# Layer 1 of a two-layer attention and Fourier kernel: token blocks 2 and 3 arrive transposed from the host instead of being turned by TensorE

## The chip, the core and the metric

The kernel runs on one core of a Trainium2 chip. The metric is the device time of one execution in microseconds (us). TensorE is called PE here, as in the profile; its weight loads are PEld. VectorE is DVE, ScalarE is ACT, GpSimd is POOL, SyncE is SP.

## What is computed

The input is one sequence of S = 2048 tokens with D = 640 features, float32, and it goes through two equal layers. With 32 heads of 20 features, one layer is

```python
x = x + attention(layernorm(x)) @ wo     # q, k, v = layernorm(x) @ wqkv
x = x + fourier(layernorm(x))            # y = Real(DFT_seq(DFT_hidden(x)))
```

`layernorm` subtracts a token's mean and divides by its standard deviation; there is no learned scale.

## The kernel before, in words

A layer has a prologue (`Qkv.prologue`, L293), an attention sweep, an output projection and a Fourier stage. The change lies in the prologue of the first layer, which takes the first 86 us.

The prologue makes what attention needs to begin: for every token the first chunk of q and k (128 of 640 columns each) and the first half of v. A product contracts over the features, so both operands need the features on the partitions. The tokens come with tokens on the partitions and must be turned. They are handled in four blocks of 512, called tb = 0 to 3, each in five chunks of 128 features, dc = 0 to 4. Float32 is kept by splitting each operand into a high and a low part: `split` (L85) lets ACT copy the source to the rounded high part (L90), and DVE then subtracts that from the source to get the low part (L91). A product of one chunk is three passes: high by high, high by low, low by high (`passes`, L100).

How a block gets ready: `load` (L146) brings 256 tokens as one tile `xa`, two for a block. `stats` (L153) lets DVE take means and variances (L121 to L124) and POOL take the power and the product (L125, L126), so that the row scale and the row bias stand in `ars`, one number per token, tokens on partitions. `norm` (L156) lets ACT normalize in place, once per 128 tokens (L130). `turn` (L164) lets PE transpose 128x128 pieces into PSUM (L167), four for a chunk, 20 for a block, and splits each chunk into `xt`.

Each engine works strictly through its own queue in the order in which the code issues to it (the schedule is manual), and waits where an operand isn't ready. The loop at L346 sets that order. For block tb it issues: the k and q products of the block (`pqk`, L103, 15 passes each; `keep` evicts them by ACT at L218 and DVE at L220 and L221 and stores them by a POOL DMA at L222); `stats` for a block further on; `turn(tb + 1)`; loads and `norm` for block tb + 2; the norms (`pn`, L230 and L231); and last, from tb = 1 on, the 60 passes of v (`pv`, L103), evicted by ACT at L263. In block 0 the v passes come ahead of `turn(1)`. So for blocks 2 and 3 the operands `xt` are made while PE works on the v passes of the block before, and PE reads them in the order dc = 0, 1, 2, 3, 4 as soon as those end. PSUM has eight banks, handed out in rotation by `bank` (L160).

SP issues the loads in the same order; after the loads of block 3 it issues the reads of q and k for the first attention step (L519, L520, L505, L506). `ones(t)` (L325) writes ones into the v tiles by POOL; the v tiles 12 to 15 are last to be used.

Of the kernel before, what the change touches and what calls it, by code (L numbers as in the profile page):

```python
# [5 lines left out]
F32 = mybir.dt.float32  # L6
F32R = mybir.dt.float32r
# [3 lines left out]
OP = mybir.AluOpType  # L11
# [25 lines left out]


@with_exitstack
def mha_fnet_kernel(ctx, tc, x_in, wqk, wv, wo, seq, hid, nat_seq, nat_hid, out):  # L40
    nc = tc.nc
    V, A, G, PE = nc.vector, nc.scalar, nc.gpsimd, nc.tensor

# [92 lines left out]
    class Qkv:  # L136
# [27 lines left out]
        def turn(s, tb, wait=False):  # L164
# [9 lines left out]
            for dc in range(ND):  # L174
# [95 lines left out]
        def begin(s, first, kq, vals, room, given):  # L270


            s.first, s.room, s.given, s.w = first, room, given, {}
# [19 lines left out]
        def prologue(s, vals, xt, fill, att):  # L293
# [31 lines left out]
            def ones(t):  # L325
                s.v[t] = vals(f"v{t}", [H * VW + 12], F32, "v")
                G.memset(s.v[t][:, :H * VW].rearrange("p (a c) -> p a c", c=VW)[:, :, DH:], 1.0)
                G.memset(s.v[t][:, H * VW:], 1.0)

            for t in range(NT - ND):  # L330
                ones(t)
            def later(tb, k, f):
                if tb + 2 < NB:
                    f(2 * tb + 4 + k)
# [11 lines left out]
            for tb in range(NB):  # L346

                sq, late, last = {}, tb == 0, tb == NB - 1
                if late:
                    for k in range(2):  # L350
                        later(tb, k, s.load)
                for k in (1, 0) if last else (0, 1):
                    p = s.bank([128, 512], "pqk")
                    for dc in range(ND):
                        for f in s.product(p, s.w[k], tb, dc):
                            f()
                    sq[k] = s.keep(p, k * ND, tb, False, (room, fill)[k])
                    if late:
                        s.stats(2 + k)
                        continue  # L360
                    later(tb, k, s.stats)
                if late:
                    for n in range(4):
                        own(tb, n)
                        if n < 2:
                            s.norm(2 + n)
                            later(tb, n, s.stats)
                if tb == 0:
                    att.setup()
# [1203 lines left out]
        banks(None)  # L1573


_INS = ["x", "wqk", "wv", "wo", "seq", "hid", "nat_seq", "nat_hid"]
_OUTS = [((S, D), "float32")]


# [16 lines left out]
def _laid_out(A_x, A_wqkv, A_wo, B_dft_seq_re, B_dft_seq_im, B_dft_hid_re, B_dft_hid_im):  # L1596
    import numpy as np

    so, do = _orders()
    w = np.asarray(A_wqkv)[do]  # L1600
    nat_seq = np.stack([np.asarray(B_dft_seq_re), np.asarray(B_dft_seq_im)])[:, so][:, :, so]
    nat_hid = np.stack([np.asarray(B_dft_hid_re), np.asarray(B_dft_hid_im)])[:, do][:, :, do]
    seq = nat_seq.reshape(2, NB, 512, NT // 2, 2, 128).transpose(1, 0, 3, 5, 4, 2)
    return {
        "x": np.asarray(A_x).reshape(S, D)[so][:, do],
        "wqk": w[:, :2 * D].reshape(ND, 128, 2 * ND, 128).transpose(2, 1, 0, 3),
        "wv": w[:, 2 * D:].reshape(ND, 128, D),
        "wo": np.asarray(A_wo)[:, do].reshape(ND, 128, D),
# [1 line left out]
        "hid": nat_hid.transpose(0, 2, 1),  # L1610
        "nat_seq": nat_seq,
        "nat_hid": nat_hid,
    }


# [23 lines left out]
```

## Time and profile before

| what | value |
|---|---|
| device time, median of 3 runs | 2447.79 us (2447.61 to 2448.09) |
| device time of the profiled execution | 2448.03 us |
| its span in the trace | 2446.2 us |
| PE busy from 8 to 86 us | 77.3 of 78 us |
| DVE busy from 8 to 86 us | 41.7 of 78 us |
| ACT busy from 8 to 86 us | 41.1 of 78 us |
| POOL busy from 8 to 86 us | 14.8 of 78 us |
| PE busy over the whole span | 99% |
| ACT busy over the whole span | 86% |

A row of the timeline reads: start in us, length in us, engine, source line, operation, output and inputs by the program's names, how many instructions are merged into the row, and in brackets how long the engine was idle before it and what ended the wait. The length of a merged row runs from the first start to the last end. A row of the groups reads: busy us in all, mean ns of one, idle time before. "SPq" is SP's queue: the length there is the time to issue, not to transfer.

### The profile page before, as it was taken

How to read it: one execution, taken by the hardware profiler on the slowest of the kernel's cores; microseconds unless marked ns; L12 is line 12 of the kernel's file. 1: busy time of each engine (PE TensorE's matmuls, PEld its weight loads, DVE VectorE, ACT ScalarE, POOL GpSimd, SP SyncE). 2: the span in 40 equal slices, each digit the busy share in tenths (PEclk: the TensorE clock that was granted, in tenths of full speed). 3: DMA queues.
4: the chain of work that ended last, by engine and by line, in shares of the span. 5: the costliest groups of instructions: out<-in, count | busy, mean ns of one | idle time of the engine just before them, and what ended most of it. 6: DMA issues, size and time to landing. Idle time of an engine off the chain costs nothing. (4 is left out here: it accounts for less than half of the span.)

```text
span 2446.2 us, 43822 instructions
## 1 busy us (share of the span) xinstructions
PE 2423.5 (99%) x16320; PEld 1168.3 (48%) x16320; DVE 995.9 (41%) x2246; ACT 2115.4 (86%) x2428; POOL 528.8 (22%) x1032
## 2 busy tenths in 40 slices
PE   8999999999999999999999999999999999999998
PEld 7644444443333332339895444454433333333496
DVE  6244442234333433427753444323433332333275
ACT  6699998899999999995457999988999999999862
POOL 2012211112212122115321212211111211222143
PEclk9999999999999999999999999999999999999999
DMA  5324231223222225318552332312221322252265
GB/s 185 101 89 127 81 113 51 77 71 108 73 93 89 89 91 162 102 39 294 188 189 96 111 103 85 118 54 70 77 83 57 92 63 70 57 153 76 77 242 198
DMA packets 128226, 262.63 MB, mean 107 GB/s; under 512 B 29936, under 2 KB 54288, under 8 KB 128004
## 3 DMA queue, kind: packets, MB, share of 16 engines
q1 hardware_dynamic: 89412, 159.89, 20.1%
q0 software_dynamic: 38592, 99.85, 12.8%
q8 instruction: 131, 2.15, 0.4%
q14 instruction: 91, 0.75, 0.1%
HBM read 175.29 MB, written 84.31 MB: 106 GB/s over the span
## 5 line engine op out<-in xcount | busy, mean ns | idle before, releaser
L544 ACT ACTIVATE e<-psc 128x1024 f32<-128x1024 f32 x2048 | 1918.0, 1060 | 108.6 <-PE psc L541 98.2
L552 PE MATMUL acc<-e,v 128*32 128x512 f32 x8192 | 1030.0, 600 | 0.4 <-DVE of L559 0.4
L541 PE MATMUL psc<-stq,stk 62*128 62x512 f32 x4096 | 746.9, 445 | 1.9 <-ACT e L544 0.5
L541 PEld LDWEIGHTS psc<-stq,stk 62*128 62x128 f32 x4096 | 334.1, 184 | 705.0 <-ACT e L544 567.5
L552 PEld LDWEIGHTS acc<-e,v 128*32 128x32 f32 x8192 | 211.1, 108 | 407.3 <-issue 369.4
L103 PE MATMUL pqk<-xt,wqk 128*128 128x512 f32 x1200 | 319.6, 407 | 0.0
L573 POOL DMA_DIRECT2D o<-oh x256 | 131.5, 522 | 825.7 <-DVE oh L568 814.0
L88 DVE CAST hl<-pqk 128x512 fp32r<-128x512 f32 x64 | 44.3, 692 | 603.4 <-PE pqk L103 603.4
L103 PEld LDWEIGHTS pqk<-xt,wqk 128*128 128x128 f32 x1200 | 213.5, 188 | 83.2 <-issue 39.6
L103 PE MATMUL pv<-wv,xt 128*128 128x320 f32 x960 | 151.7, 313 | 0.0
L103 PEld LDWEIGHTS pv<-wv,xt 128*128 128x128 f32 x960 | 141.0, 188 | 13.5 <-issue 9.7
L559 DVE STREAM_TRANSPOSE of<-acc 128x512 f32<-128x512 f32 x64 | 45.8, 715 | 226.3 <-PE acc L552 226.3
L573 POOL DMA_DIRECT2D o<-ot x256 | 128.6, 509 | 1.8 <-issue 0.9
L222 POOL DMA_DIRECT2D scrk<-hl x40 | 27.8, 694 | 412.5 <-DVE hl L91 251.9
L222 POOL DMA_DIRECT2D scrq<-hl x40 | 28.3, 708 | 404.9 <-DVE hl L91 239.8
L96 PE MATMUL py<-wo,o 128*128 128x320 f32 x320 | 101.0, 315 | 0.0
L822 DVE TENSOR_REDUCE far<-cq 128x1 f32<-128x512 f32 (+5 forms) x169 | 98.5, 584 | 5.7
L98 PE MATMUL py<-wo,o 128*128 128x320 f32 x320 | 98.7, 308 | 0.0
L97 PE MATMUL py<-wo,o 128*128 128x320 f32 x320 | 98.7, 308 | 0.0
L826 DVE TENSOR_TENSOR cq<-cq 128x512 f32<-128x512 f32 (+4 forms) x166 | 96.4, 581 | 3.7 <-DMA cq<-in_nat_seq_dram 3.3
L261 DVE COPY v<-pv 128x320 f32<-128x320 f32 x32 | 15.7, 489 | 161.2 <-PE pv L103 161.2
L231 DVE TENSOR_REDUCE top<-pn 32x1 f32<-32x512 f32 x50 | 33.7, 676 | 76.7 <-PE pn L230 76.5
(204 smaller groups left out, 1758.5 us busy)
## 6 DMA issues: line engine op xcount, KB each, us to landing
cq<-in_nat_seq_dram POOLq DMA_DIRECT2D x64, 512.0 KB, 5.3
scrq<-hl POOLq DMA_DIRECT2D x40, 512.0 KB, 3.2
scrk<-hl POOLq DMA_DIRECT2D x40, 512.0 KB, 3.1
stq<-scrq SPq DMA_DIRECT2D x256, 80.0 KB
stk<-scrk SPq DMA_DIRECT2D x128, 160.0 KB
o<-o SPq DMA_DIRECT2D x32, 384.0 KB
stq<-scrq SPq DMA_DIRECT2D x256, 40.0 KB
stk<-scrk SPq DMA_DIRECT2D x128, 80.0 KB
```

Source lines behind the costliest of these rows:

```text
L96: PE.matmul(out_ap, ah, bh, start=start, stop=False)
L97: PE.matmul(out_ap, ah, bl, start=False, stop=False)
L98: PE.matmul(out_ap, al, bh, start=False, stop=stop)
L103: yield lambda i=i, j=j, k=k: PE.matmul(out_ap, a[i], b[j], start=dc == 0 and k == 0, stop=dc == ND - 1 and k == 2)
L222: G.dma_start(s.scr["qk"[k]][c * 128:(c + 1) * 128, :, tb * 512:(tb + 1) * 512], hl.bitcast(F32))
L541: PE.matmul(p[:, i], s.k[g, kc // 8, j][r, kc % 8 * 128:(kc % 8 + 1) * 128], s.q[g, qb, j][r], start=True, stop=True)
L544: A.activation(e, p, AF.Exp, scale=SCALE)
L552: PE.matmul(s.acc[32 * j:32 * j + 32], s.a.v[kc][:, v0:v0 + 32], s.e[n, j // 2][:, j % 2], start=kc == 0, stop=kc == NT - 1, skip_group_ch ...
L559: V.transpose(t0.rearrange("p b c -> p (b c)"), s.acc)
L573: G.dma_start(s.o[k, h * DH:(h + 1) * DH, qb * 512:(qb + 1) * 512], hl[k][32 * j:32 * j + DH])
L822: V.tensor_reduce(to, x, op=OP.max, axis=AX.X, apply_absolute_value=True)
L826: V.tensor_tensor(y, x, y, op=op)
```

## The change

The host adds an input `x_turned`, the tokens of the second half of the sequence (blocks 2 and 3), with features on the first axis. In the first layer only (`host`, which is true where the source is the input `x_in`), blocks 2 and 3 are no longer normalized by ACT and turned by PE.

- `row` (new, in the place of `norm` for blocks 2 and 3): SP writes the row scales and biases of the block to DRAM, four DMAs of 256 single numbers, then reads them back spread over all 128 partitions as two tiles `row` of 512 numbers each, then loads the block's part of `x_turned` by four DMAs into the two tiles that had held the block's tokens (1.3 MB for a block; the tokens themselves are still loaded for the statistics).
- `spread` (new, in the place of `turn(2)` and `turn(3)`): for each chunk POOL multiplies by the scale row, DVE adds the bias row, ACT copies the high part, DVE subtracts for the low part. The fifth chunk lies in two halves of 256 tokens, so a block has six steps.
- The `row` tiles live where v tiles 12 to 15 will be, so the ones for these four are written after block 3 is spread.

```diff
+        def row(s, k):
+            tb, j = divmod(k, 2)
+            if j == 0:
+                s.stat = dr.tile([2, 512], F32, name=f"stat{tb}_{s.L}")
+            for i in range(2):
+                nc.sync.dma_start(s.stat[i, j * 256:(j + 1) * 256].rearrange("(n p) -> p n", p=128), s.rs[k][:, i],
+                                  single_packet=False)
+            if j == 0:
+                return
+            s.rows = [s.vals(f"v{NT - 1 - 2 * (tb - 2) - i}", [512], F32, "row") for i in range(2)]
+            for i in range(2):
+                nc.sync.dma_start(s.rows[i], s.stat[i:i + 1].to_broadcast([128, 512]))
+            s.turned = [(s.first if n % 4 < 2 else s.room)(f"x{n % 4}", [2 * D], F32, "xturned") for n in (k - 1, k)]
+            src = x_turned.rearrange("c p t -> p c t")[:, :, (tb - 2) * 512:(tb - 1) * 512]
+            for i, t in enumerate(s.turned):
+                nc.sync.dma_start(t[:, :1024].rearrange("p (c t) -> p c t", c=2), src[:, 2 * i:2 * i + 2])
+                nc.sync.dma_start(t[:, 1024:], src[:, ND - 1, i * 256:(i + 1) * 256])
+
+        def spread(s, tb):
+            for dc in range(ND):
+                x = s.xtp(f"xt{tb}_{dc}", [2, 512], F32R, "xt")
+                s.xt[tb, dc] = [x[:, 0], x[:, 1]]
+                whole = [(s.turned[dc // 2][:, dc % 2 * 512:(dc % 2 + 1) * 512], slice(0, 512))] if dc < ND - 1 else \
+                    [(t[:, 1024:], slice(256 * i, 256 * i + 256)) for i, t in enumerate(s.turned)]
+                for y, cols in whole:
+                    G.tensor_tensor(y, y, s.rows[0][:, cols], op=OP.mult)
+                    V.tensor_tensor(y, y, s.rows[1][:, cols], op=OP.add)
+                    split(x[:, 0, cols], x[:, 1, cols], y)
...
                 elif tb == 1:
-                    for t in range(NT - ND, NT):
+                    for t in range(NT - ND, NT - 4 if host else NT):
                         ones(t)
                 if tb + 1 < NB:
-                    s.turn(tb + 1)
+                    (s.spread if host and tb else s.turn)(tb + 1)
                     for k in range(2):
                         later(tb + 1, k, s.load)
+                if tb == 2 and host:
+                    for t in range(NT - 4, NT):
+                        ones(t)
                 for k in range(1 if last else 0, 2):
-                    later(tb, k, s.norm)
+                    later(tb, k, s.row if host else s.norm)
                     s.norms(s.bank, k * ND, tb, sq[k])
```

In the changed kernel the lines behind the new functions are 31 to 36 higher (L222 is L253, L263 is L294). Three places show how the queues change.

DVE, where block 2 is made ready (behind the statistics of block 3, ahead of the evictions of block 2), before:

```order
L123 TENSOR_SCALAR ars<-amv 128x2
L124 TENSOR_SCALAR ars<-amv 128x2
L91 TENSOR_TENSOR xt<-ptr,xt 128x512 x5
L231 TENSOR_REDUCE top<-pn 32x1
L221 TENSOR_TENSOR hl<-pqk,hl 128x512
```

The same place now, with the tiles' numbers (520 and 521 are the two tiles of turned tokens, 517 is the bias row, 607, 612 and 617 the first three of the five chunks):

```order
L124 TENSOR_SCALAR ars_593<-amv_592 128x2
L213 TENSOR_TENSOR xturned_520<-xturned_520,row_517 128x512
L91 TENSOR_TENSOR xt_607<-xturned_520,xt_607 128x512
L213 TENSOR_TENSOR xturned_520<-xturned_520,row_517 128x512
L91 TENSOR_TENSOR xt_612<-xturned_520,xt_612 128x512
L213 TENSOR_TENSOR xturned_521<-xturned_521,row_517 128x512
L91 TENSOR_TENSOR xt_617<-xturned_521,xt_617 128x512
```

The row goes on so: five subtractions on end have become six pairs of an addition and a subtraction (the last two of half the size), and each subtraction reads a tile that ACT writes between the two.

POOL, from the statistics of block 3 to the block after, now (scrk and scrq are the stores of k and q; 516 is the scale row of block 2, 644 that of block 3):

```order
L125 TENSOR_TENSOR ars_593<-ars_593,powers_97 128x2
L126 TENSOR_TENSOR ars_593<-ars_593 128x2
L358 MEMSET v_604 128x32
L359 MEMSET v_604 128x12
L212 TENSOR_TENSOR xturned_520<-xturned_520,row_516 128x512 x2
L212 TENSOR_TENSOR xturned_521<-xturned_521,row_516 128x512 x2
L212 TENSOR_TENSOR xturned_520<-xturned_520,row_516 128x256
L212 TENSOR_TENSOR xturned_521<-xturned_521,row_516 128x256
L253 DMA scrq_0_67<-hl_748 256x1x512
L253 DMA scrk_0_68<-hl_770 256x1x512
L212 TENSOR_TENSOR xturned_648<-xturned_648,row_644 128x512 x2
L212 TENSOR_TENSOR xturned_649<-xturned_649,row_644 128x512 x2
```

Before, the two stores followed the statistics with nothing but the ones between; now the six multiplications of block 2 stand ahead of them, and those of block 3 behind.

SP, from the second half of block 3's loads to the reads for attention, now (368 and 400 are the row scales and biases of the two halves of block 2):

```order
L151 DMA xa_506<-in_x_dram 128x2x640
L191 DMA stat2_0_508<-ars_368 128x2x1 x2
L191 DMA stat2_0_508<-ars_400 128x2x1 x2
L197 DMA row_516<-stat2_0_508 128x512
L197 DMA row_517<-stat2_0_508 128x512
L201 DMA xturned_520<-in_x_turned_dram 128x2x512
L202 DMA xturned_520<-in_x_turned_dram 128x256
L201 DMA xturned_521<-in_x_turned_dram 128x2x512
L202 DMA xturned_521<-in_x_turned_dram 128x256
L555 DMA stq_450<-scrq_0_67 40x1x512
```

Ten DMAs have come in ahead of the reads for attention, and the two that fill the rows read what the four ahead of them write. Ten more for block 3 follow the q reads.

More of the change, by code (lines that the diff above doesn't have):

```diff
@@ L39, in mha_fnet_kernel @@
 @with_exitstack
-def mha_fnet_kernel(ctx, tc, x_in, wqk, wv, wo, seq, hid, nat_seq, nat_hid, out):
+def mha_fnet_kernel(ctx, tc, x_in, wqk, wv, wo, seq, hid, nat_seq, nat_hid, x_turned, out):
     nc = tc.nc
@@ L270, in begin @@
         def begin(s, first, kq, vals, room, given):
-            s.first, s.room, s.given, s.w = first, room, given, {}
+            s.first, s.room, s.given, s.w, s.vals = first, room, given, {}, vals
             for k in range(2):
@@ L331, in prologue @@
                 ones(t)
+            host = s.src is x_in
             def later(tb, k, f):
@@ L1573, in mha_fnet_kernel @@
         banks(None)
-_INS = ["x", "wqk", "wv", "wo", "seq", "hid", "nat_seq", "nat_hid"]
+_INS = ["x", "wqk", "wv", "wo", "seq", "hid", "nat_seq", "nat_hid", "x_turned"]
 _OUTS = [((S, D), "float32")]
@@ L1600, in _laid_out @@
     w = np.asarray(A_wqkv)[do]
+    x = np.asarray(A_x).reshape(S, D)[so][:, do]
     nat_seq = np.stack([np.asarray(B_dft_seq_re), np.asarray(B_dft_seq_im)])[:, so][:, :, so]
@@ L1604, in _laid_out @@
     return {
-        "x": np.asarray(A_x).reshape(S, D)[so][:, do],
+        "x": x,
         "wqk": w[:, :2 * D].reshape(ND, 128, 2 * ND, 128).transpose(2, 1, 0, 3),
@@ L1612, in _laid_out @@
         "nat_hid": nat_hid,
+        "x_turned": x.T.reshape(ND, 128, S)[:, :, S // 2:],
     }
```

## Prediction

> **What bounds the kernel now.** I read the page's first part first, then the timeline of PE over the stage that the change touches.
>
> ```profile
> PE 2423.5 (99%) x16320; PEld 1168.3 (48%) x16320; DVE 995.9 (41%) x2246; ACT 2115.4 (86%) x2428; POOL 528.8 (22%) x1032
> ...
> 39.26 2.35 PE L167 MATMUL ptr<-ident,xa 128*128 128x128 f32 x20
> 41.53 0.39 PE L230 MATMUL pn<-sq,ind 128*32 128x512 bf16 x1
> 41.85 9.07 PE L103 MATMUL pv<-wv,xt 128*128 128x320 f32 x60
> 50.76 7.00 PE L103 MATMUL pqk<-xt,wqk 128*128 128x512 f32 x30
> 57.59 2.34 PE L167 MATMUL ptr<-ident,xa 128*128 128x128 f32 x20
> 59.87 0.39 PE L230 MATMUL pn<-sq,ind 128*32 128x512 bf16 x1
> 60.19 9.07 PE L103 MATMUL pv<-wv,xt 128*128 128x320 f32 x60
> 69.09 6.99 PE L103 MATMUL pqk<-xt,wqk 128*128 128x512 f32 x30
> ...
> 85.83 1.40 PE L541 MATMUL psc<-stq,stk 62*128 62x512 f32 x6
> ```
>
> PE is busy for 99% of the span, and between 39.26 us and the first attention scores at 85.83 us no row has an idle time in brackets. PE sets the end of this stage, and attention follows on the same queue, so every us that PE gains or loses here arrives at the end of the kernel. Look at where PE reads a prepared block: block 2 at 50.76, behind the v passes of block 1 (41.85), and block 3 at 69.09. The 30 passes of a block take 7.00 us, 0.231 us a pass, so block 2's first 15 end at 54.2 and all 30 at 57.7.
>
> **What is removed.** Two sets of 20 transposes. Each holds PE from its start to the next row: 41.53 - 39.26 = 2.27 us, and 59.87 (the norm's start) less 57.59, 2.28 us. That is 4.55 us in all and the most that the change can gain. ACT loses eight normalizations (the groups of ACT in the first 86 us, with busy us, mean ns and idle us ahead):
>
> ```profile
> L130 ACT ACTIVATE xa<-xa,ars 128x640 f32<-128x640 f32 x16 | 13.8, 928 | 3.1 <-POOL ars L126 3.1
> L90 ACT ACTIVATE xt<-ptr 128x512 fp32r<-128x512 f32 x20 | 10.2, 619 | 0.2 <-PE ptr L167 0.2
> L90 ACT ACTIVATE wqk<-wraw 128x640 fp32r<-128x640 f32 x2 | 1.5, 728 | 0.4 <-DMA wraw<-in_wqk_dram 0.4
> L90 ACT ACTIVATE wv<-wvraw 128x320 fp32r<-128x320 f32 x5 | 2.3, 472 | 0.5 <-DMA wvraw<-in_wv_dram 0.5
> L263 ACT ACTIVATE v<-pv 128x320 f32<-128x320 f32 x16 | 6.9, 435 | 19.7 <-PE pv L103 19.6
> ```
>
> Eight at 0.93 us are 7.4 us, worth nothing: ACT waits for PE here (19.6 us ahead of the evictions of v), not PE for ACT.
>
> **What is added: a chain of four engines in the place of PE.** For each chunk POOL multiplies, DVE adds, ACT copies, DVE subtracts, and by the order on DVE the next addition stands behind that subtraction. The ACT copy reads SBUF: 728 ns for 640 elements and 472 for 320 give 0.63 us for 512, 0.42 for 256 (the PSUM form, 619, agrees). The two DVE operations read two SBUF tiles, as L569 does in the groups of the whole span; POOL's price comes from its groups and from two rows of its timeline in the Fourier stage:
>
> ```profile
> L569 DVE TENSOR_TENSOR ot<-ot,oh 128x512 f32<-128x512 f32 x64 | 44.3, 692 | 2.2
> L213 DVE TENSOR_TENSOR sqh<-hl 128x256 bf16<-128x256 f32 x48 | 20.1, 420 | 0.8
> L126 POOL TENSOR_TENSOR ars<-ars 128x2 f32<-128x2 f32 x16 | 3.1, 195 | 1.3
> 1225.43 0.74 POOL L1300 TENSOR_TENSOR xd<-xd,r 128x319 f32<-128x319 f32 x1
> 1226.14 0.75 POOL L1299 TENSOR_TENSOR xd<-xd,r 128x321 f32<-128x321 f32 x1
> ```
>
> DVE: 0.69 us for 512 elements, 0.42 for 256. POOL: 0.195 us for 2 elements and 0.74 for 319, so 1.72 ns an element: 1.07 us for 512, 0.63 for 256; back to back such instructions start 0.71 apart at 0.74 long, so little is hidden. One whole step alone is 0.69 + 0.63 + 0.60 (the next addition starts some 0.09 before a subtraction ends) + 0.05 for two hand-overs = 1.97 us, a half step 1.2 us. Six steps take 4 x 1.97 + 2 x 1.2 = 10.3 us behind the first multiplication; from its start, 1.07 more, 11.4. Before, DVE was through with a block in 3.07 us (the row of 44.06, below).
>
> **POOL and DVE get in each other's way.** The Fourier stage runs the same two kinds side by side; these are its DVE timeline, three rows, and its POOL timeline, two:
>
> ```profile
> 1196.39 0.48 DVE L1299 TENSOR_TENSOR xd<-xd,r 128x321 f32<-128x321 f32 x1
> 1196.79 1.04 DVE L1300 TENSOR_TENSOR xd<-xd,r 128x319 f32<-128x319 f32 x1
> 1217.43 0.48 DVE L1300 TENSOR_TENSOR xd<-xd,r 128x319 f32<-128x319 f32 x1
> 1196.62 0.87 POOL L1299 TENSOR_TENSOR xd<-xd,r 128x321 f32<-128x321 f32 x1 [3.63 <-DVE r L1291]
> 1197.44 1.12 POOL L1300 TENSOR_TENSOR xd<-xd,r 128x319 f32<-128x319 f32 x1
> ```
>
> The DVE addition of 319 elements takes 0.48 us alone (1217.43) and 1.04 at 1196.79: POOL's ends at 1197.49, DVE's 0.34 later at 1197.83. POOL's next, begun at 1197.44, ends at 1198.56, 0.73 behind DVE's end: it took 1.12 where 0.74 is the rule. Neither ran during the other; they took turns, and POOL with its next instruction ready did not keep DVE out. So while multiplications are left, each DVE operation waits for up to one of them. The Trainium skill, page "SBUF — State Buffer", section "Who interferes with whom", says it as an exclusive lock: a DVE instruction with two SBUF inputs and a GpSimd instruction that reads SBUF exclude each other, and the later one blocks until the first is done. The trace agrees (1.04 against 0.48); without that rule the sum below would be 5.3 us lower.
>
> Stepping through block 2 by turns (start of POOL = 0; multiplications 1.07 and 0.63; a DVE operation holds for 0.34 x 512 / 319 = 0.54, or 0.27): the low parts of chunks 0 to 4 are ready at 4.3, 7.7, 9.7, 11.6 and 14.1 us. Two steps are slowed, then POOL is through; the turns cost 2.7 us against the 11.4.
>
> **When does POOL start?** Its own queue says: behind the statistics of block 3. The timelines of DVE (three rows) and POOL (three) at that place:
>
> ```profile
> 43.99 0.16 DVE L124 TENSOR_SCALAR ars<-amv 128x2 f32<-128x2 f32 x1
> 44.06 3.07 DVE L91 TENSOR_TENSOR xt<-ptr,xt 128x512 fp32r<-128x512 f32 x5
> 55.55 0.69 DVE L221 TENSOR_TENSOR hl<-pqk,hl 128x512 fp32r<-128x512 f32 x1 [7.83 <-ACT sq L218]
> 44.97 0.20 POOL L126 TENSOR_TENSOR ars<-ars 128x2 f32<-128x2 f32 x1
> 60.65 0.68 POOL L222 DMA_DIRECT2D scrk<-hl  x1 [3.42 <-ACT xt L90]
> 61.21 0.66 POOL L532 MEMSET zeros<- 32x512 f32 x1
> ```
>
> The product L126 starts at 44.97 and one pair of ones is left, so 45.2. The data must be there by then. Below: SP's issues, the packets moved in the us from 1025 and in the us from 1026, and two one-us windows, whose last number is GB/s:
>
> ```profile
> 31.92 0.92 SPq L151 DMA_DIRECT2D xa<-in_x_dram  x2
> 32.93 0.92 SPq L519 DMA_DIRECT2D stq<-scrq  x1
> 80.78 0.26 SPq L470 DMA_DIRECT2D shiftb<-sh  x1
> 82.33 1.11 SPq L527 DMA_DIRECT2D stq<-shiftb  x4
> ...
> 1022.93 2.63 SPq L1169 DMA_DIRECT2D mid<-in_seq_dram  x4
> DMA packets 716, 0.24 MB, mean 239 GB/s; under 512 B 544, under 2 KB 697, under 8 KB 715
> DMA packets 524, 0.03 MB, mean 30 GB/s; under 512 B 504, under 2 KB 523, under 8 KB 523
> 32.00:33.00 1.00, 1.00 (x5) 0.69 (x5) 1.00 (x3) 1.00 (x3) 0.00 (x0) 1.00 0.12 15
> 36.00:37.00 1.00, 1.00 (x7) 0.81 (x6) 0.00 (x0) 1.00 (x3) 0.00 (x0) 1.00 1.00 391
> ```
>
> SP is free for the four scatters at 32.93. Four DMAs of 256 single numbers exist at 1022.93 (the reverse way, into SBUF): 0.66 us to issue each, and some 1000 packets below 512 B went in the two us from 1025. So issue ends at 35.6, block 3's tokens fill the queues to about 37 (391 GB/s at 36), the packets end at 39, and with the lag of the write of 80.78, whose reader went at 82.33, the rows are read from about 39.5. Two reads and the first turned load at 0.46 us each (31.92, two in 0.92), a us to first data (15 GB/s in the us from 32), then 1 MB at 0.39 MB/us: there at about 44, one us ahead of POOL. I take 45.2 and keep up to 3 us of delay for the range: no row shows 4-byte writes to DRAM. On these the Trainium skill, page "DMA: Bandwidth & Descriptors", section "Specifications", says that a transfer below 512 B is a read-modify-write, so below line rate; were each packet to take twice the time, the data would come at about 46 and the sum would be 0.8 us higher, an estimate from that page that no run here shows.
>
> **Block 2.** The last low part is ready at 45.2 + 14.1 = 59.3, two passes follow (0.46): the first 15 passes end at 59.8, not at 54.2. **+5.5 us**, the removed transposes already counted: PE would be there at 48.5.
>
> **Block 3.** Let T be the end of block 2's passes. Before, T = 57.7, POOL was free behind the store of k at 61.2, T + 3.5, and block 3's first 15 passes ended at 69.09 + 3.46, T + 14.9. Now POOL starts at T + 3.5 again (statistics are over; the store L222 stands ahead), the last low part comes at T + 17.6, the passes end at T + 18.1. **+3.2 us.** The data is no issue: SP gets to block 3's rows at about 48 and needs some 10 us, T is 63.
>
> **What lies beside other work.** The evictions of v on ACT and the norm's reduction on DVE now stand behind the chain, and the stores on POOL too; nobody waits: the eight banks rotate, and none of those v passes' banks is asked for before the next block's products are done. The reads of q and k on SP come 9 to 11 us later (32.93 to about 42); attention needs them at 85.83. The ones for four v tiles wait for the last addition; their evictions come some 8 us later. If one of these covers fails, it costs its own length, a us or two.
>
> **Sum.** 5.5 + 3.2 = 8.7 us, on the profiled execution's 2448.03 us (0.24 above the median of the runs, 1.8 above its span): **2456.7 us**.
>
> **Rivals.** (1) No turns, as if POOL and DVE didn't meet: the chain is 11.4 instead of 14.1, so +2.8 and +0.5, 2451.3 us. Against it stand the rows at 1196. (2) POOL keeps DVE out until its six are done (5.4 us), then 10.4 us: 15.8 a block, +12.1 in all, 2460.1. Against it: DVE got in at 1197.49 with POOL's next waiting. (3) The data or POOL is later: each us adds one us to block 2 alone, and a multiplication of 1.28 us instead of 1.07 (from the 0.87 of 1196.62) would add 2.2: 2459 to 2462. For it: nothing here has scattered to DRAM. (4) Not slower: the chain hides behind the v passes and only the transposes' 4.55 us show, 2443.5. It decides at one point: chunk 4 must be ready when PE asks, 48.5 + 4 x 0.69 = 51.3, 6.1 us behind POOL's start. For it: DVE has nothing to do for 7.83 us ahead of 55.55. Against it: 14.1 by the rows, and each step needs DVE twice with ACT between.
>
> **How the numbers follow.** Forecast by turns 0.62; rival 2 or 3, 0.22; rival 1, 0.13; rival 4, 0.03. The range takes in rival 1's end and the late cases: 2451 to 2462. A measurement here can tell 0.2%, 4.9 us, from no change: 2443.1 to 2452.9. Rival 4 lies within it, rival 1 too, and the low end of the forecast touches it: same 0.16, slower 0.83, faster 0.01 (4.55 us is the most).
>
> **What would show it.** PE should be idle ahead of L103 `pqk` behind DVE `xt`, about 8 us before block 2 (from 48.5) and 5 to 6 before block 3; L212 should take 1.07 us first, then more, L213 1 us or more in its first two; the first scores should start at about 94.5. If L213 stays at 0.69, rival 1 holds; if POOL waits for DMA, rival 3. I am wrong altogether if PE shows no idle time there.

## The result, and the profile after

The changed kernel takes **2475.92 us** (median of 4 runs, 2474.12 to 2478.22), the kernel before 2447.94 us (2447.61 to 2448.74): a ratio of 1.0115, interval 1.0103 to 1.0128. The forecast was 2456.7, the range 2451 to 2462. Slower was right, the size was not: 28.0 us were lost where 8.7 were expected. The profiled execution took 2474.98 us, its span is 2472.8, 26.6 above the span before. In the changed kernel the chain's lines are L212 (GpSimd's multiplication), L213 (VectorE's addition) and L90/L91 (copy and subtraction); the store of q and k is L253, the scatters are L191, the reads of the rows L197.

The timeline of PE over the stage shows where all of it arises:

```profile
39.48 9.06 PE L103 MATMUL pv<-wv,xt 128*128 128x320 f32 x60
58.09 0.80 PE L103 MATMUL pqk<-xt,wqk 128*128 128x512 f32 x1 [9.55 <-ACT xt L90]
...
68.61 7.05 PE L103 MATMUL pqk<-xt,wqk 128*128 128x512 f32 x18 [0.81 <-ACT xt L90]
75.59 0.39 PE L261 MATMUL pn<-sq,ind 128*32 128x512 bf16 x1
75.91 9.07 PE L103 MATMUL pv<-wv,xt 128*128 128x320 f32 x60
86.94 0.50 PE L103 MATMUL pqk<-xt,wqk 128*128 128x512 f32 x1 [1.96 <-ACT xt L90]
...
95.66 7.17 PE L103 MATMUL pqk<-xt,wqk 128*128 128x512 f32 x18 [0.80 <-ACT xt L90]
...
113.18 1.05 PE L577 MATMUL psc<-stq,stk 62*128 62x512 f32 x6 [0.53 <-ACT v L294]
```

The first attention scores start at 113.18 us and not at 85.83: 27.35 us later, which is the whole loss (by the spans 0.7 us comes back further on). Block 2's products end at about 75.66 in the place of 57.7, 18.0 later. Block 3's end at 102.83 in the place of 76.08, so block 3 adds 8.75; the last 0.6 lies at attention's start, where TensorE waits 0.53 us for ScalarE's last eviction of v. Three things in these rows and behind them were not in the sum, or not in that size.

**GpSimd starts block 2 late.** Four views of the changed kernel: SP's timeline, SP's waits from 30 to 60 us, the packets moved from 36 to 38 and from 44 to 46 us, and POOL's timeline.

```profile
32.73 2.30 SPq L191 DMA_DIRECT2D stat<-ars  x4
46.60 0.81 SPq L197 DMA_DIRECT2D row<-stat  x2
```

```profile
SPq L197 <- DMA stat<-ars: 11.5, 1, 11.5
```

```profile
DMA packets 1201, 0.25 MB, mean 126 GB/s; under 512 B 1104, under 2 KB 1104, under 8 KB 1201
DMA packets 15, 0.06 MB, mean 31 GB/s; under 512 B 0, under 2 KB 0, under 8 KB 15
```

```profile
54.35 7.65 POOL L212 TENSOR_TENSOR xturned<-xturned,row 128x512 f32<-128x512 f32 x6 [6.52 <-DMA xturned<-in_x_turned_dram]
78.56 0.68 POOL L253 DMA_DIRECT2D scrk<-hl  x1 [5.37 <-DMA stk<-scrk]
79.15 6.52 POOL L212 TENSOR_TENSOR xturned<-xturned,row 128x512 f32<-128x512 f32 x6
```

The four scatters are issued by 35.03, and the records have 1104 packets below 512 B between 36 and 38, so as a stream of packets they are through in two us. Yet SP waits 11.5 us more for them to have landed, the last of it with 31 GB/s moving in all. Everything behind that wait follows late: rows at 46.60, turned tokens after them, GpSimd at 54.35 where 45.2 was forecast, **9.15 us**. GpSimd had been free from 47.83 and waited for that DMA.

**The clock falls.** A row has a stretch in us, its length, the busy us of PE, PEld, DVE, ACT and POOL with their instructions, the granted clock of TensorE (1.00 is full speed), the share of the DMA and GB/s; the clock is the last but two:

```profile
39.00:48.00 9.00, 9.00 (x61) 8.62 (x60) 4.27 (x15) 1.09 (x2) 2.61 (x7) 1.00 1.00 113
53.00:54.00 1.00, 0.00 (x0) 0.00 (x0) 0.00 (x0) 0.00 (x0) 0.00 (x0) 0.92 1.06 403
54.00:72.00 18.00, 11.31 (x20) 5.80 (x21) 10.71 (x14) 5.75 (x12) 7.65 (x6) 0.50 0.31 68
74.00:75.00 1.00, 1.00 (x5) 0.83 (x4) 0.00 (x0) 0.00 (x0) 0.00 (x0) 0.84 0.98 300
87.00:88.00 1.00, 0.78 (x2) 0.42 (x3) 1.00 (x2) 0.00 (x0) 0.00 (x0) 0.98 0.00 0
90.00:99.00 9.00, 8.11 (x16) 4.33 (x16) 6.37 (x13) 4.49 (x10) 0.92 (x9) 0.50 0.02 4
```

PE is idle from 48.54. A mean of 0.92 between 53 and 54 puts the fall to 0.50 at 53.84, and 0.84 between 74 and 75 puts the return at 74.3, 5.7 us into the passes that run without a gap from 68.61. In block 3 it falls once more, at 88.0. So the 18 passes at 68.61 take 7.05 us, 0.39 a pass, where a pass took 0.231, and those at 95.66 take 7.17. Against the 4.58 and 4.51 us of e3_warm (below), where the clock stays at 1.00, that is **2.5 and 2.7 us**.

**Block 3's first addition is kept out.** The timeline of DVE, two rows of block 2 and one of block 3:

```profile
55.64 1.73 DVE L213 TENSOR_TENSOR xturned<-xturned,row 128x512 f32<-128x512 f32 x1 [8.93 <-POOL xturned L212]
58.97 1.76 DVE L213 TENSOR_TENSOR xturned<-xturned,row 128x512 f32<-128x512 f32 x1
80.59 5.63 DVE L213 TENSOR_TENSOR xturned<-xturned,row 128x512 f32<-128x512 f32 x1 [2.57 <-DMA stk<-scrk]
```

In block 2 VectorE gets its turn between multiplications (1.73 and 1.76 us, then 0.68 once GpSimd is through). In block 3 the first addition lasts 5.63 us and ends at 86.22, behind the end of GpSimd's last (79.15 + 6.52 = 85.67). (The bracket names the event that came last ahead of it; the operand it needs is GpSimd's first product.) The chain is 16.9 us long in block 3 (79.15 to 96.07) and 14.67 in block 2 (54.35 to 69.02), against 14.1: **+2.8 and +0.6 us**.

Sum by these terms: block 2 5.5 + 9.15 + 0.6 + 2.5 = 17.75 (18.0 seen), block 3 3.2 + 2.8 + 2.7 = 8.7 (8.75 seen), and 0.6 at attention's start. A sum that fits is no proof; the experiments take the terms apart.

### The profile page after: what moved, and what is told of

Its sections match the earlier page's. It is cut to its first block, busy times and chain, and to the rows that moved or that the text cites. A ratio compares the mean times of both kernels' runs of the same rounds, so it can differ in the third digit from the quotient of the medians.

```text
span 2472.8 us, 43813 instructions
## 1 busy us (share of the span) xinstructions
PE 2433.7 (98%) x16280; PEld 1170.5 (47%) x16280; DVE 1011.3 (41%) x2260; ACT 2109.9 (85%) x2422; POOL 542.0 (22%) x1044
## 5 line engine op out<-in xcount | busy, mean ns | idle before, releaser
L103 PE MATMUL pqk<-xt,wqk 128*128 128x512 f32 x1200 | 334.5, 419 | 15.8 <-ACT xt L90 14.5
L103 PEld LDWEIGHTS pqk<-xt,wqk 128*128 128x128 f32 x1200 | 218.6, 193 | 108.9 <-issue 39.6
L253 POOL DMA_DIRECT2D scrq<-hl x40 | 28.3, 707 | 406.5 <-DVE hl L91 240.1
L253 POOL DMA_DIRECT2D scrk<-hl x40 | 27.7, 693 | 405.4 <-DVE hl L91 252.3
```

The costliest lines, as they stand in the source:

```text
L103: yield lambda i=i, j=j, k=k: PE.matmul(out_ap, a[i], b[j], start=dc == 0 and k == 0, stop=dc == ND - 1 and k == 2)
L253: G.dma_start(s.scr["qk"[k]][c * 128:(c + 1) * 128, :, tb * 512:(tb + 1) * 512], hl.bitcast(F32))
```

## The experiments

The runs of the kernel before that go with them have medians of 2447.53 to 2447.77 us. Line numbers shift with each kernel's edit; GpSimd's multiplication and VectorE's addition are named by `xturned<-xturned,row`.

### e1_no_scatter: the scatters taken away

```
-            for i in range(2):
-                nc.sync.dma_start(s.stat[i, j * 256:(j + 1) * 256].rearrange("(n p) -> p n", p=128), s.rs[k][:, i],
-                                  single_packet=False)
...
-                nc.sync.dma_start(s.rows[i], s.stat[i:i + 1].to_broadcast([128, 512]))
+                nc.sync.dma_start(s.rows[i], x_turned[i, 0:1, 0:512].to_broadcast([128, 512]))
```

> Left out: the four scatters of row scales to DRAM per block; the two rows are read from another place in DRAM, so the normalization uses wrong numbers. Theory A (the wait of 11.5 us for the scattered 4-byte writes sets when the chain of block 2 begins): POOL's first multiplication of block 2 starts at 45 to 46 us instead of 54.35, DVE's wait of 2.9 us at the statistics of block 3 goes, and the time falls by 9 to 12 us to 2464 to 2467. Rival B (the 1.3 MB of turned tokens behind the rows is what comes late): the first multiplication still starts after 50 us and the time stays above 2471.

Measured: 2466.96 us (2465.36 to 2467.95), ratio 1.0080 (1.0063 to 1.0097); 9.0 us of the 28 are gone. POOL's timeline, one row, PE's, one row of block 2, and DVE's, one row of block 3:

```profile
44.59 7.75 POOL L209 TENSOR_TENSOR xturned<-xturned,row 128x512 f32<-128x512 f32 x6
```

```profile
58.95 6.27 PE L103 MATMUL pqk<-xt,wqk 128*128 128x512 f32 x18 [0.80 <-ACT xt L90]
```

```profile
70.16 5.63 DVE L210 TENSOR_TENSOR xturned<-xturned,row 128x512 f32<-128x512 f32 x1 [2.59 <-POOL xturned L209]
```

GpSimd starts at 44.59, waiting for nothing: with the scatters gone the data is in time, as the prediction had assumed for the kernel with them. Block 3's addition still takes 5.63 us, and the clock still falls (block 2's 18 passes take 6.27 us, with no gap of TensorE longer than 1.61 us ahead of them), so these are not the scatters' doing.

### e2_half_packets: the same bytes in half as many packets

```
-                nc.sync.dma_start(s.stat[i, j * 256:(j + 1) * 256].rearrange("(n p) -> p n", p=128), s.rs[k][:, i],
-                                  single_packet=False)
+                nc.sync.dma_start(s.stat[i, j * 256:(j + 1) * 256].rearrange("(p n) -> p n", p=128), s.rs[k][:, i])
```

Each scatter is 128 packets of 8 bytes in the place of 256 of 4. The flag `single_packet=False` goes with the old form; no run here changes the one without the other.

> Left out: the order of the tokens within the rows (each partition's two numbers are written side by side, so the rows are permuted); there are 128 packets of 8 bytes in a scatter instead of 256 of 4. Theory A1 (each small write costs the DMA engine a fixed time, about 10 us for 64 packets an engine, 0.15 us each): the wait of the row reads for the scatters falls from 11.5 us to about 6, POOL's first multiplication of block 2 comes at about 49, the time falls by 5 to 6 us to about 2470. Rival A2 (a fixed delay of the write, or of its place behind the loads of block 3, whatever the number of packets): the wait stays above 10 us and the time above 2474.

Measured: 2470.65 us (2470.04 to 2474.52), ratio 1.0098 (1.0081 to 1.0115). SP's timeline, and the packets from 36 to 38 us:

```profile
32.83 2.13 SPq L191 DMA_DIRECT2D stat<-ars  x4
41.25 0.81 SPq L196 DMA_DIRECT2D row<-stat  x2
```

```profile
DMA packets 682, 0.23 MB, mean 117 GB/s; under 512 B 592, under 2 KB 592, under 8 KB 682
```

From the end of issue to the reads of the rows it is 6.3 us (34.96 to 41.25) and not 11.6 (35.03 to 46.60): 512 packets fewer save 5.3 us, some 10 ns each, with the same number of bytes, and the wait lies behind the records of the packets, which end by 38 in both kernels. GpSimd starts at 49.19. So the wait goes with the packets (or with the flag) and not with the bytes, but not with the packets alone: block 3's scatters wait 9.3 us in the changed kernel (58.99 to 68.25) and 3.6 here (56.02 to 59.64), and in e4_resync block 2's 1024 packets took 10.3 us.

### e3_warm: filler products where TensorE would wait

```
+            def warm(n, new=False):
+                if new:
+                    s.hot = s.bank([128, 512], "pwarm")
+                for _ in range(n):
+                    PE.matmul(s.hot, s.w[0][:, 0, 0], s.xt[0, 0][0], start=True, stop=True)
...
+                        if host and tb >= 2 and k == (1 if last else 0) and dc < ND - 1:
+                            warm(5)
...
+                    if host and not last:
+                        warm(40 if tb == 1 else 8, True)
```

> Added: matmuls whose result nobody reads, on PE while it waits: 40 of 128x512 ahead of block 2's products, 8 ahead of block 3's, 5 behind each of the first four chunks. Theory C (PE's granted clock falls to 0.5 after about 5 us without work, 0.39 us a pass instead of 0.23, and that costs 2.7 us in each of the two blocks): the granted clock stays at 1.0 through both blocks, block 2's second 15 passes take 3.5 us instead of about 6, and the time falls by 5 us to 2470 or 2471. Rival (the slower passes come from waits for chunks that the trace does not resolve): no change, 2474 to 2478, or slower by the added matmuls.

Measured: 2468.25 us (2467.78 to 2468.71), ratio 1.0085 (1.0068 to 1.0101), 7.7 us below the changed kernel. Its windows, one row of PE and one of DVE in block 3:

```profile
48.00:72.00 24.00, 22.22 (x92) 16.41 (x91) 10.97 (x14) 5.76 (x12) 8.12 (x7) 1.00 0.42 113
72.00:96.00 24.00, 24.00 (x125) 20.24 (x124) 13.71 (x19) 7.21 (x15) 10.45 (x18) 1.00 0.52 172
```

```profile
68.27 4.58 PE L103 MATMUL pqk<-xt,wqk 128*128 128x512 f32 x18
```

```profile
77.91 1.77 DVE L213 TENSOR_TENSOR xturned<-xturned,row 128x512 f32<-128x512 f32 x1 [2.70 <-POOL xturned L212]
```

The clock stays at 1.00 and the 18 passes take 4.58 us: work that is thrown away makes the kernel faster. 7.05 - 4.58 and 7.17 - 4.51 are 5.1 us for both blocks. Most of the rest of the 7.7 is block 3's addition, which got its turn here (1.77) and so made the chain 2.1 us shorter; 0.5 is block 2's data, which came earlier (GpSimd starts at 53.89). GpSimd began block 3 0.15 us behind the store's end here (76.58, the store ending at 76.43), not at it. So this run moved two terms, and the next two separate the second.

### e4_resync and e7_store_ahead: what stands directly ahead of the multiplications

In e4_resync two tiny instructions of GpSimd stand between the store and block 3's multiplications. In e7_store_ahead, made from e4_resync, block 2 gets a store there, behind its data, and block 3 keeps the two tiny instructions:

```
+            if tb == 3:
+                z = s.room("sync", [2], F32, "sync")
+                G.memset(z[:, 0:1], 0.0)
+                G.tensor_copy(z[:, 1:2], z[:, 0:1])
```

```
+            z = s.room("sync", [2], F32, "sync")
+            if tb == 3:
+                G.memset(z[:, 0:1], 0.0)
+            else:
+                G.tensor_copy(z[:, 0:1], s.turned[1][:, 1279:1280])
+                spare = dr.tile([128, 2], F32, name="spare")
+            G.tensor_copy(z[:, 1:2], z[:, 0:1])
+            if tb == 2:
+                G.dma_start(spare, z)
```

> Added: two tiny POOL instructions ahead of block 3's multiplications, the second of which waits for the first to complete. Theory D (in block 3 the store issued by POOL just ahead leaves GpSimd's cores out of step, so that its six multiplications, back to back, never leave the shared port free and DVE's first addition takes 5.63 us; when all begin together POOL and DVE take turns as in block 2): DVE's first addition of block 3 takes about 1.7 us, the chain of block 3 14.7 us instead of 16.9, and the time falls by 2 to 2.5 us to about 2473.5. Rival D2 (who gets in is decided by something else, such as how close the requests lie): the first addition still takes over 5 us and the time stays at 2475 to 2476.

> The kernel e4_resync, and block 2 gets on GpSimd what block 3 had in the changed kernel: when the turned tokens are in, a small copy, then a store issued by GpSimd's queue, and directly behind it the six multiplications. Theory D (a store directly ahead lets the multiplications run so closely that the first addition gets no turn): block 2's first addition takes about 5.6 us in the place of 1.7, the chain about 17 us in the place of 14.7, and the time is 2 to 3 us above e4_resync's, 2475.5 to 2477 us. Rival (the starved addition belongs to something else at block 3's place, such as the work of TensorE and ScalarE there): the first addition stays at 1.7 us and the time within 1 us of e4_resync's.

Measured: e4_resync 2473.56 us (2472.56 to 2477.03), ratio 1.0110 (1.0093 to 1.0127); e7_store_ahead 2477.88 us (2477.60 to 2478.20), ratio 1.0124 (1.0107 to 1.0141). POOL and DVE of e4_resync at block 3, then of e7_store_ahead at block 2:

```profile
78.31 0.18 POOL L209 COPY sync<-sync 128x1 f32<-128x1 f32 x1
78.47 7.77 POOL L216 TENSOR_TENSOR xturned<-xturned,row 128x512 f32<-128x512 f32 x6
```

```profile
79.78 1.77 DVE L217 TENSOR_TENSOR xturned<-xturned,row 128x512 f32<-128x512 f32 x1 [2.87 <-POOL xturned L216]
```

```profile
56.01 0.60 POOL L214 DMA_DIRECT2D spare<-sync  x1 [0.29 <-DMA stq<-scrq]
56.63 6.28 POOL L221 TENSOR_TENSOR xturned<-xturned,row 128x512 f32<-128x512 f32 x6
```

```profile
57.94 5.52 DVE L222 TENSOR_TENSOR xturned<-xturned,row 128x512 f32<-128x512 f32 x1 [12.24 <-POOL xturned L221]
```

With a copy ahead, VectorE takes turns and GpSimd's six last 7.77 us; with a store ahead, GpSimd's six run through in 6.28 and the first addition takes 5.52 us. It can be put into either block, so it belongs to the order on GpSimd and not to the place. The chain of e4_resync's block 3 is 14.8 us (78.47 to 93.25) where it was 16.9, that of e7_store_ahead's block 2 is 16.7 (56.63 to 73.30) where it was 14.7. These chains are the evidence, more than the times: those of e4_resync overlap with the changed kernel's, and 0.8 us of its gain is an earlier start of block 2 (53.51 against 54.35). The time of e7_store_ahead came out 0.9 us above what was expected, since GpSimd starts 3 us later than in e4_resync as well (56.63 against 53.51). Why a store ahead does it stays open; the rows only show that it does.

### e5_all_three: scatters gone, clock kept, turns in both blocks

The edits of e1_no_scatter, e3_warm (2 fillers ahead of block 2 in the place of 40) and e4_resync together.

> Three things at once: the row scales and biases are not scattered (the rows are read from the turned tokens, so the normalization is left out), filler products keep TensorE busy where it would wait for a spread block, and GpSimd starts block 3's multiplications behind two small instructions of its own in the place of the store. Theory (late data, the fallen clock and block 3's starved addition are everything that the prediction missed): what is left is the prediction's own 8.7 us, so 2456 to 2459 us; GpSimd starts block 2 at about 44.6 us, the granted clock is 1.00 in every window, no first addition takes 5.6 us, and the first attention scores start at about 95. Rival (the three are not independent, or a fourth cost stands behind them): 2462 us or more, with the rest showing as idle time of TensorE in one place.

Measured: 2459.72 us (2459.37 to 2460.55), ratio 1.0051 (1.0034 to 1.0067), 0.7 us above the expected band, 3.0 above the forecast. Two rows of PE:

```profile
59.08 4.58 PE L103 MATMUL pqk<-xt,wqk 128*128 128x512 f32 x18
96.34 1.40 PE L588 MATMUL psc<-stq,stk 62*128 62x512 f32 x6
```

Block 2's first 15 passes end at 59.8 (three of the 18 behind 59.08), where the forecast had them to the tenth. That agreement is in part luck: GpSimd starts at 44.68 and not 45.2, and the chain is 14.8 us and not 14.1. The scores start 10.5 us later than before, not 8.7: the chain is 14.8 us in each block, GpSimd starts block 3 0.4 later behind its two tiny instructions, and the 18 passes with the wait for the last low part among them take 4.6 us each time. With the three terms gone, what is left at the scores is the prediction's own sum and 1.8 us. The other 1.7 of the 12.2 us lie behind the first scores, and their cause stays open.

### e6_add_in_psum and e9_two_banks: additions that don't meet GpSimd

```
+            low, p = [s.bank([128, 512], name) for name in ("plow", "pnew")]
+            A.activation(low, s.rows[1], AF.Copy)
...
-                    V.tensor_tensor(y, y, s.rows[1][:, cols], op=OP.add)
-                    split(x[:, 0, cols], x[:, 1, cols], y)
+                    V.tensor_tensor(p[:, cols], y, low[:, cols], op=OP.add)
+                    split(x[:, 0, cols], x[:, 1, cols], p[:, cols])
```

This is e9_two_banks, made from the changed kernel; e6_add_in_psum, made from e5_all_three, took a new bank for each chunk.

> The kernel e5_all_three, and the addition keeps out of SBUF as far as it can: ScalarE copies the row of biases to a PSUM bank, VectorE adds it to the multiplied chunk and writes the sum to another bank, and the copy and the subtraction read it there, so that no VectorE instruction of the chain reads two SBUF tiles (normalization left out as in e5_all_three). Theory P (additions and subtractions wait because GpSimd's and VectorE's two-input SBUF instructions exclude each other): every addition takes about 0.7 us whether GpSimd runs or not, a block's chain falls from about 14.7 to about 11.2 us, and the time is 5 to 7 us below e5_all_three's, 2450 to 2453 us. Rival (the waits come from the order and the hand-overs between the engines): additions still take 1.7 us and more while GpSimd runs, and the time stays within 2 us of e5_all_three's.

> The changed kernel with one edit: the addition keeps out of SBUF as in e6_add_in_psum, but only two PSUM banks a block serve it (one for the row of biases, one for the sums of all chunks), so that the v passes find their banks free. Theory P (the exclusion of two-input SBUF instructions makes the chain long, in block 3 most of all): additions take about 0.7 us in both blocks, each chain falls to about 11.9 us (from 14.7 and 16.9), GpSimd starts block 2 at 54.4 as in the changed kernel, and the time falls by 2.8 + 5.0 us to about 2468 us (2466 to 2470). Rival (the six banks that e6_add_in_psum took were not what held the v passes, and the ring holds them here too): TensorE waits ahead of the v passes as there, and the time is above the changed kernel's 2475.9 us.

Measured: e6_add_in_psum 2486.20 us (2485.75 to 2487.31), ratio 1.0158 (1.0141 to 1.0175), far from what was expected; e9_two_banks 2467.43 us (2466.31 to 2468.44), ratio 1.0082 (1.0065 to 1.0099), in the expected band. Of e6_add_in_psum a row each of POOL, DVE and PE:

```profile
44.99 6.31 POOL L216 TENSOR_TENSOR xturned<-xturned,row 128x512 f32<-128x512 f32 x6
```

```profile
48.27 0.69 DVE L217 TENSOR_TENSOR pnew<-xturned,plow 128x512 f32<-128x512 f32 x1
```

```profile
56.12 9.47 PE L103 MATMUL pv<-wv,xt 128*128 128x320 f32 x45 [10.54 <-DVE pnew L217]
```

The mechanism came out as stated: with one operand in PSUM, an addition takes 0.69 us in the middle of GpSimd's run, and the chain falls to 11.85 us (44.99 to 56.84). The time did not: the v passes come next in the ring of eight banks, and six banks were held until the chain's end, so PE waited 10.54 us where it had been busy. With two banks that wait is gone. Of e9_two_banks a row of POOL and one of DVE in block 3, and a subtraction of block 2:

```profile
76.07 6.53 POOL L214 TENSOR_TENSOR xturned<-xturned,row 128x512 f32<-128x512 f32 x6
```

```profile
77.52 0.70 DVE L215 TENSOR_TENSOR pnew<-xturned,plow 128x512 f32<-128x512 f32 x1 [2.58 <-POOL xturned L214]
```

```profile
55.96 0.69 DVE L91 TENSOR_TENSOR xt<-pnew,xt 128x512 fp32r<-128x512 f32 x1 [0.66 <-ACT xt L90]
```

A store stands directly ahead here too, and the first addition takes 0.70 us: both the turns and the 5.6 us come from the two engines meeting in SBUF. The sum's output goes to PSUM here as well, but the subtraction, which writes SBUF as before and only reads one operand elsewhere, takes 0.69 us while GpSimd multiplies (53.30 to 59.62), where it took 0.98 in the changed kernel; so it is the second input that counts. The chains are 12.6 and 12.8 us; one shared bank costs 0.2 us a step against e6_add_in_psum. That the time lies in the band is partly luck: the chains save 6.2 us and not the 7.8 expected, and the rest is block 2's data, which came 1.05 us earlier (53.30), and block 3's slow passes, which cost 1.25 less (5.92 us for the 18).

### e8_block3_alone and e10_block3_mended: one block only

```
-                    (s.spread if host and tb else s.turn)(tb + 1)
+                    (s.spread if host and tb == 2 else s.turn)(tb + 1)
...
-                    later(tb, k, s.row if host else s.norm)
+                    later(tb, k, s.row if host and tb else s.norm)
```

e10_block3_mended adds the edit of e9_two_banks and packets of 8 bytes, `rearrange("(p n) -> p n", n=2)` without the flag, whose rows are read through the view `"q (j p n) -> q j n p"`.

> Block 2 is normalized by ScalarE and transposed on TensorE as before the change; only block 3 comes turned and is spread. Theory (each block pays by itself; the scatters' 10 us delay only block 2, since block 3's are issued early enough to be nearly hidden): block 2's products end at 57.7 us as before, block 3 pays its chain and the fallen clock, 7 to 11 us in all, 2454 to 2459 us, so block 2 alone holds about 20 of the 28 us. Rival (what is lost at block 3 is the echo of block 2's delay): within 5 us of the kernel before, 2452 us or less.

> The mended version of the smaller change: block 3 alone is spread (as e8_block3_alone), the addition goes through two PSUM banks (as e9_two_banks), and the scales are scattered as 128 packets of 8 bytes and read back in the order in which they lie, so that the normalization is the reference's. Theory (the chain's length and the start of its data set the price of block 3): the data is there at about 61 us, behind GpSimd's store, the chain takes 11.9 us and block 3's first 15 passes end about 1 us later than in the kernel before; with a part of the fallen clock 2448.5 to 2451 us, against 2455.7 for e8_block3_alone. Rival (the fallen clock is most of block 3's price and stays): 2452 us or more.

Measured: e8_block3_alone 2455.73 us (2454.57 to 2456.49), ratio 1.0032 (1.0020 to 1.0043); e10_block3_mended 2451.95 us (2451.37 to 2453.11), ratio 1.0017 (1.0008 to 1.0027). POOL and PE of the first, then of the second:

```profile
62.82 2.55 POOL L212 TENSOR_TENSOR xturned<-xturned,row 128x512 f32<-128x512 f32 x2 [1.82 <-DMA xturned<-in_x_turned_dram]
```

```profile
77.26 7.23 PE L103 MATMUL pqk<-xt,wqk 128*128 128x512 f32 x18 [0.81 <-ACT xt L90]
94.24 1.10 PE L577 MATMUL psc<-stq,stk 62*128 62x512 f32 x6
```

```profile
60.98 6.60 POOL L220 TENSOR_TENSOR xturned<-xturned,row 128x512 f32<-128x512 f32 x6
```

```profile
73.35 5.95 PE L103 MATMUL pqk<-xt,wqk 128*128 128x512 f32 x18 [1.60 <-ACT xt L90]
89.05 0.97 PE L585 MATMUL psc<-stq,stk 62*128 62x512 f32 x6
```

Block 3 by itself costs 8.4 us at the first scores (94.24 against 85.83), so its price is no echo of block 2's delay, and block 2 holds the other 20 of the 28. That it is nearly the 8.75 of the changed kernel is chance: here GpSimd waits 1.82 us for the data, and its first addition gets its turn (1.77 us, a chain of 14.85) in the place of the 16.9. In e10_block3_mended the data is in time (GpSimd starts right behind its store) and the chain is 12.8 us; 3.2 us are left at the first scores, with the 18 passes still at 0.33 us each: 5.95 us against the 4.51 of e3_warm, 1.4 of the 3.2. The time lies 1 us above the theory's band and just short of its rival's 2452, so it doesn't decide between the two; the chain had been put at 11.9 and is 0.9 longer.

### e11_both_mended: the whole change with both mends

> The whole change with the same two mends: both blocks spread, additions through two PSUM banks, scatters in packets of 8 bytes read back in their own order (the normalization is the reference's). Theory (the costs add up): the changed kernel's 2475.9 less 7.8 us for the chains and 5.3 us for the packets, 2463 us (2460 to 2466): still slower than before, because block 2's data comes at about 49 us and its chain takes 12 us where TensorE wants the first chunk at 48.5 us. Rival (one of the mends hides the other): 2468 us or more.

Measured: 2464.44 us (2463.39 to 2465.36), ratio 1.0070 (1.0053 to 1.0087), in the expected band. POOL's timeline:

```profile
48.78 2.52 POOL L220 TENSOR_TENSOR xturned<-xturned,row 128x512 f32<-128x512 f32 x2 [3.70 <-PE pv L103]
52.04 3.92 POOL L220 TENSOR_TENSOR xturned<-xturned,row 128x512 f32<-128x512 f32 x4 [0.74 <-DMA stq<-scrq]
```

Block 2's multiplications begin at 48.78, when PE is already through with its v passes. (The bracket names those passes because they end about then; in e1_no_scatter the multiplications start at 44.59 while they run, so it is the data that is waited for.) No version run here beats the kernel before; the nearest is e10_block3_mended. The transposes that a further version could still save are 4.55 us, 0.19%.

## Why the prediction was wrong

- **What bounds the kernel, what is removed, what is hidden: right.** PE's timeline carried the whole loss to the end; ACT's eight normalizations gave nothing, and the later q and k reads cost nothing that shows. Not in the sum are the 0.53 us that the first scores wait for the last eviction of v on ACT; why they wait here and not in the kernel before stays open.
- **"When does POOL start?": the step that failed.** It let the packets end at 39 us and the rows be read from 39.5. The packets do end by 38; the reads went at 46.60. The price of the scatter was taken from packets of 4 bytes read into SBUF, and the records of packets were taken for the landing. Written to DRAM, 1024 packets landed 11.6 us after their issue and 512 of twice the size 6.3, some 10 ns for each packet less. The prediction named this as unknown ("no row shows 4-byte writes to DRAM") and bounded it at 3 us, though nothing bounded it there. By e1_no_scatter it is worth 9.0 us.
- **Left out: the clock.** The prediction gave PE 8 idle us and priced its passes at 0.231 us throughout. Between 48.54 and 54 the clock fell to 0.50, and both blocks paid 2.5 us and more; e3_warm kept the clock and took 5.1 us away. The Trainium skill, page "TensorE: Matmul & The Clock Gate", Part 1 on the clock gate, has the clock at half once TensorE has been idle for a window of about 3.4 us (5.2 us behind the last matmul in its example) and at full rate again after about 3.4 us of sustained work. The changed kernel's fall in block 2, 5.3 us behind the last matmul, fits that; over the runs it came from 2.2 (e9_two_banks, 48.55 to 50.77) to 5.3 us behind it, so the nearness to the example is chance. The return took 5.7 us, and over the runs the clock came back from 3.0 to 6.2 us into the 18 passes (e7_store_ahead, 72.89 to 75.87 and 96.97 to 103.18). Block 3's fall came at 88.0 with no gap longer than 1.96 us. There the measurement decides. Nor would the rule have given the missing term from the prediction's own idle time, which comes in pieces between the chunks: in e1_no_scatter, where block 2's data is in time as forecast, no gap is longer than 1.61 us, and the clock fell at 52.7 all the same. What makes it fall there stays open.
- **Block 2's chain by turns: right.** 14.67 us against 14.1, with the two slowed additions where they were stepped. A multiplication of 512 takes 1.25 us from one to the next and not 1.07; two of them lie ahead of the first addition's end, which is most of the 0.6. Rival 3's 1.28 us was the nearer price, but with turns in both blocks (e5_all_three) a chain is 0.7 us longer, 1.4 in all and not its 2.2.
- **Block 3's chain: rival 2 came true there, and not in block 2.** POOL kept DVE out until its six were done; 16.9 us, +2.8. The forecast had one order for both blocks, and the store directly ahead of block 3's multiplications, which it named for POOL's start, made the difference (e4_resync, e7_store_ahead). GpSimd's start at T + 3.5 was right: 79.15 with T at 75.66.
- **The exclusion: shown.** e9_two_banks takes the second SBUF operand away and both effects go. (Rival 1 lies 5.4 us below the forecast; the prediction's sentence on the rule has 5.3.) The Trainium skill, page "SBUF — State Buffer", section "Who interferes with whom", says that a VectorE instruction with at most one SBUF input, outside its two-port modes, doesn't contend with GpSimd. The trace agrees, 0.70 us against 1.73 and 5.63.
- **The range.** Rivals 2 and 3 were each held to be alone and at most 14 us; they came together, with the clock beside them: the late data in block 2, the addition kept out in block 3, and slow passes behind PE's waits in both.

## What to carry to other kernels

This chain through DRAM was late by its landing, not by its packets: where one number a partition must become a row, count packets and look for the wait of the reader, not for the end of the records. Where PE is the bound, a wait costs more than its length if the passes behind it run slow: here about 2.5 us a block, with gaps of 1.6 us too (e1_no_scatter, e8_block3_alone). Price the passes behind a PE that works in pieces, and try filler products. Where a GpSimd instruction with two SBUF inputs runs beside VectorE ones with two, the price depends on who gets in next: give VectorE an operand in PSUM, and check whose banks that takes.

## What the runs showed of the hardware that was not expected

- 1024 writes of 4 bytes to DRAM, recorded as done within 2 us, landed 11.6 us after issue; 512 of 8 bytes 6.3 us. In the last part of the 11.6 us the DMA moved 31 GB/s in all (44 to 46 us).
- The clock also falls without a long gap: in e8_block3_alone no idle stretch of block 3 is longer than 1.61 us, and the 18 passes at 77.26 still take 7.23 us, 0.40 a pass. It comes back 3.0 to 6.2 us into those passes (e7_store_ahead), so the price differs from block to block.
- With both inputs of the addition in SBUF, six multiplications of GpSimd take 7.65 to 7.82 us when VectorE gets its turns between them, and 6.28 to 6.53 when it doesn't; VectorE got no turn in the four blocks where a store of GpSimd's queue ends as they begin, and got it in the eleven others.
